# A long-convolution block and a gated FFN on one core: block 2's spectrum by n mod 4, warm-up products on a constant, diagonals by VectorE, the last rows in three pieces

## The chip, the cores and the metric

The kernel runs on one core of a Trainium2 chip. The metric is the device time of one execution in microseconds (us), taken on the device. Three runs of the kernel before gave 263.92, 263.94 and 264.01 us; the median is 263.94. Beside these there is one profiled execution, from which all rows below come.

The engines are named as the profile names them: PE is TensorE (matrix products; PEld is its loading of weights), DVE is VectorE, ACT is ScalarE, POOL is GpSimd, SP is SyncE, which mostly issues DMAs. A queue in a row such as SPq or POOLq is the engine's DMA-issuing side. L337 is line 337 of the kernel.

## The reference

Inputs are q, k, v of 2048 x 640, a four-tap kernel per channel, a long kernel `ssm_k` of 640 x 2048, a per-channel weight `ssm_D`, and the three matrices of a gated FFN with 1728 hidden columns. All are bfloat16.

```
kv = shift_conv4(k) * v                       # four taps along the sequence, per channel
y  = causal_conv(kv, ssm_k) + kv * ssm_D      # length 2048, by real FFT of length 4096
h  = q + layernorm(q) * y
n  = layernorm(h)
out = h + (silu(n @ w_gate) * (n @ w_up)) @ w_down
```

## The kernel before

The sequence is cut into four blocks of 512 positions, numbered 0 to 3. A block's 512 rows lie as four interleaved groups: position 4p + r is partition p, group r (r = 0 to 3). The causal convolution of length 2048 is done block by block: the spectrum X_j of block j's `kv` and the spectrum G_j of block j of `ssm_k` (each a real transform of 512 values to length 1024) are made once as matrix products with a constant basis `WF`; H_j is a window of G_j and G_(j-1); the output block j is the inverse transform of the sum over i of X_i times H_(j-i).

The stages of block j are named, in the code, Lg, Lk, Lv, Lx (loads), g (transpose of `ssm_k`), G (its spectrum), h (window), k (the four-tap convolution and the product with v), X (its spectrum), m0 to mj (complex products and sums, on VectorE), n (statistics of the first layer norm), i (inverse transform, the product with the normed q, the sum h and the second norm's statistics), t (the normed rows, turned), and f (the FFN). The name is followed by the block, so X2 is the spectrum of block 2's `kv` and m22 is X_2 times H_0.

**A spectrum** (`transform`, L353). In the form "sub", each of four column groups c takes four row groups r with two halves of 320 columns: 8 products of 128x128 by 128x320 (L337) into one PSUM tile, evicted twice (L326: the even rows doubled, and the sum), and one subtraction over the whole width (L372) gives the other half of the frequencies. In the form "four" the symmetry of n mod 4 is used once more: for each of even and odd rows only two column groups are multiplied, with two row groups each (4 products a group), also evicted twice; the other two groups follow by half-width subtractions (L401, one each for even and odd), and two full-width operations (L405 for the difference, L408 for the sum) join even and odd. Where the name is in `ADDLO` the sum is a DMA that adds into its target, issued by POOL (L410, through `add_into`, L257). Which form a spectrum takes stands in the table `SUM`; a name in `DIRECT` takes neither, but a path with a further constant `minus`. Inverse transforms i2 and i3 have the form "four" too.

**The FFN** of a block (`ffn`, L865) takes the turned normed rows hT: gate and up products (L889 for whole groups of 256 hidden columns, L923 for the odd rest), Silu and a copy on ScalarE (L906, L912; L931, L932), their product on VectorE (L914, L933), and the down products (L956): per group of 128 rows 14 chunks by two halves of 320 columns. For blocks 0 to 2 the rows are copied by ScalarE and added to `out` by POOL's DMAs (L963); block 3 adds h on VectorE (L972; L974 for halves) and SP stores the result (L976). The very last group of 128 rows is done as two halves of 320 columns, both in one PSUM tile `ps` (L950), each with its own eviction and store.

**The start.** VectorE and POOL make an identity (L983, L986). TensorE runs 14 products of the identity with itself to warm up (`spin`, L990), turns the taps (L1002), runs 16 more, then transposes block 0's k (L529), runs 8 more and does the four-tap convolution as products with diagonal matrices (L554), 80 of them, 20 for each r. The 20 diagonals (five chunks c of 128 channels, four taps each) are the identity times a tap (L1010): chunks 0 to 2 by VectorE, 3 and 4 by POOL.

**The order.** Every operation is added to a `Plan` by the code's loops, with the engine, an assumed duration, and the buffers that it reads and writes, and so gets a number. The list `ORDER` then says in which order they are emitted. Each engine carries out its own operations in that order, and so do the DMA queues of SP, ScalarE and POOL. A negative number ~n means the operation n in its other form, mostly an eviction by VectorE in place of ScalarE. Buffers (`SLOTS`) are given out and taken back in this order too, so a load waits for the last reader of the buffer that it gets. `schedule` (L174) only checks and emits; the list itself was made by a search outside the kernel with the assumed durations (`Plan.TOOK` for DMAs by packet size, the numbers in `pe`, `act`, `dve`, and 660 for a transposing DMA, a "turn").

TensorE's queue mixes two kinds of work: that of the convolution of block j, which depends on VectorE, and the FFN of block j-1, which only needs its weights and hT.

Of the kernel before, what the change touches and what calls it, by code (L numbers as in the profile page):

```python
# [10 lines left out]
FP32 = mybir.dt.float32  # L11
BF16 = mybir.dt.bfloat16
# [35 lines left out]
SUM = {'X3': 'four', 'i2': 'four', 'i3': 'four', 'G3': 'four', 'G0': 'four'}  # L48
# [7 lines left out]
PAIRED = True  # L56
ORDER = [
# [75 lines left out]
class Plan:  # L133
    TOOK = {8: 9, 128: 13, 256: 18, 512: 28.5, 640: 33, 1024: 47, 1280: 57, 4096: 160, 5120: 199}
# [63 lines left out]
def kernel(ctx: ExitStack, tc: tile.TileContext, A_q, A_k, A_v, A_shift_k, A_ssm_k, A_ssm_D, B_x,  # L198
# [53 lines left out]
    def transfer(nbytes, fn, r, w):  # L252
        return plan.moved("turn", nbytes, 256, fn, r, w)
# [161 lines left out]
    def g_turned(g, drow=None):  # L415
# [19 lines left out]
        if drow:  # L435
            dve(480, lambda: nc.vector.tensor_add(ap(gT)[0:1, 0, :], ap(gT)[0:1, 0, :], ap(drow)[0:1, :]), [drow], [(gT, 0)])
# [82 lines left out]
    def turned_k(k, behind=None, table=None):  # L519
        if plan.block in KTURN:  # L520
            return k
# [343 lines left out]
    def ffn(j, hT, h, end=False, lead=0):  # L865
# [73 lines left out]
        for gi in range(lead, NGRP - 1):  # L939
            chunks((gi,), ROWS)  # L940
# [207 lines left out]
```

## Time and profile before

| | |
|---|---|
| median of three runs | 263.94 us (263.92 to 264.01) |
| the profiled execution's own time | 264.02 us |
| its span, first to last instruction | 262.3 us |
| TensorE clock granted | 1.00 in all slices |
| mean DMA rate over the span | 166 GB/s |
| SP's queue, share of 16 DMA engines | 56.2% |
| POOL's queue, share of 16 DMA engines | 14.7% |

How to read the rows. A row of instructions has start and duration in us, engine, line, operation, the tile written and read with shapes, a count, and in brackets the time the engine stood idle before it with what ended that. A row of groups has busy time in us and mean ns of one, then idle time before. A row of waits has the total us, the number and the longest. A row of the chain has start, us and what ran. The 40 digits are the span in equal slices of 6.56 us, in tenths. Durations of products are latencies and overlap; how fast they follow one another is read from the chain.

### The profile page before, as it was taken

How to read it: one execution, taken by the hardware profiler on the slowest of the kernel's cores; microseconds unless marked ns; L12 is line 12 of the kernel's file. 1: busy time of each engine (PE TensorE's matmuls, PEld its weight loads, DVE VectorE, ACT ScalarE, POOL GpSimd, SP SyncE). 2: the span in 40 equal slices, each digit the busy share in tenths (PEclk: the TensorE clock that was granted, in tenths of full speed). 3: DMA queues.
4: the chain of work that ended last, by engine and by line, in shares of the span. 5: the costliest groups of instructions: out<-in, count | busy, mean ns of one | idle time of the engine just before them, and what ended most of it. 6: DMA issues, size and time to landing. Idle time of an engine off the chain costs nothing.

```text
span 262.3 us, 4671 instructions
## 1 busy us (share of the span) xinstructions
PE 255.3 (97%) x1786; PEld 159.5 (61%) x1802; DVE 204.9 (78%) x296; ACT 168.4 (64%) x288; POOL 67.4 (26%) x84
## 2 busy tenths in 40 slices
PE   7999999999999999999999999999999999999994
PEld 7977786554665567755754467544447764444772
DVE  4589999999999999999999999999998401115022
ACT  3999999986495896668968887343696033434100
POOL 4440000029972300025050000599900022000000
PEclk9999999999999999999999999999999999999999
DMA  7999999728958999759998769699190498000003
GB/s 257 342 260 309 235 343 297 134 62 154 292 108 155 196 266 162 127 122 279 238 174 218 183 151 169 105 235 237 51 225 1 80 205 139 7 0 0 2 0 100
DMA packets 72066, 43.42 MB, mean 166 GB/s; under 512 B 30886, under 2 KB 69100, under 8 KB 72044
## 3 DMA queue, kind: packets, MB, share of 16 engines
q1 hardware_dynamic: 68066, 37.22, 56.2%
q0 software_dynamic: 3968, 5.90, 14.7%
q8 instruction: 14, 0.23, 0.4%
q14 instruction: 8, 0.07, 0.1%
q10 hardware_dynamic: 10, 0.01, 0.0%
HBM read 30.01 MB, written 4.59 MB: 132 GB/s over the span
## 4 chain that ended last, share of the span: by engine, by line
PE 92%; DVE 2%; DMA 2%; ACT 2%; issue 1%; POOL 0%
PE ps L889 39%; PE ps L956 23%; PE ps L337 12%; PE ps L554 6%; PE ps L779 5%; PE ps L923 5%; DMA out_dram<-big 2%; PE ps L995 2%; PE ps L529 1%; ACT S L326 1%; PE ps L432 1%; DVE row L793 1%; DVE big L806 0%; ACT big L828 0%; DVE row L974 0%
## 5 line engine op out<-in xcount | busy, mean ns | idle before, releaser
L889 PE MATMUL ps<-big,big 128*128 128x512 bf16 x465 | 106.9, 379 | 0.8
L889 PEld LDWEIGHTS <-big 128*128 128x128 bf16 x480 | 46.8, 98 | 52.3
L956 PE MATMUL ps<-wd,tT 128*128 128x320 bf16 x416 | 60.4, 299 | 0.8 <-DVE row L974 0.8
L956 PEld LDWEIGHTS <-tT 128*128 128x128 bf16 x416 | 40.7, 98 | 17.3 <-issue 1.0
L906 ACT ACTIVATE sg<-ps 128x1024 bf16<-128x1024 f32 (+1 forms) x28 | 26.8, 961 | 30.1 <-PE ps L889 26.6
L337 PE MATMUL ps<-big,WF 128*128 128x320 bf16 x240 | 39.6, 299 | 0.5 <-ACT big L326 0.2
L914 DVE TENSOR_TENSOR tT<-sg,sg 128x1024 bf16<-128x1024 bf16 (+1 forms) x25 | 16.0, 644 | 26.1 <-ACT sg L912 26.1
L645 DVE TENSOR_TENSOR S<-S,big 128x2560 bf16<-128x2560 bf16 x23 | 34.3, 1492 | 0.8
L644 DVE TENSOR_TENSOR big<-S,S 128x2560 bf16<-128x2560 bf16 x23 | 34.1, 1485 | 0.0
L337 PEld LDWEIGHTS <-WF 128*128 128x128 bf16 x240 | 23.2, 98 | 12.8 <-issue 1.6
L912 ACT CAST sg<-ps 128x1024 bf16<-128x1024 f32 (+1 forms) x25 | 23.5, 945 | 7.1 <-PE ps L889 6.8
L963 POOL DMA_DIRECT2D out_dram<-row x12 | 11.0, 1038 | 60.2 <-ACT row L962 60.2
L655 ACT ACTIVATE row<-big 128x640 bf16<-128x640 bf16 x32 | 23.7, 744 | 1.4 <-DVE big L806 1.1
L326 ACT CAST S<-ps 128x320 bf16<-128x320 f32 (+1 forms) x38 | 20.0, 575 | 3.2 <-PE ps L337 3.0
L554 PE MATMUL ps<-diag,kT 128*128 128x128 bf16 x320 | 19.0, 219 | 0.0
L554 PEld LDWEIGHTS <-kT 128*128 128x128 bf16 x320 | 18.3, 98 | 1.0 <-DVE kT L533 0.2
L326 ACT ACTIVATE big<-ps 128x640 bf16<-128x640 f32 (+1 forms) x25 | 15.7, 666 | 4.8 <-PE ps L337 4.7
L962 ACT CAST row<-ps 128x640 bf16<-128x640 f32 x12 | 8.3, 690 | 14.2 <-PE ps L956 10.7
L257 POOL DMA_DIRECT2D S<-big x2 | 2.6, 1296 | 57.5 <-DVE big L639 30.7
L708 ACT ACTIVATE row<-big,sm 128x640 bf16<-128x640 bf16 x19 | 17.1, 939 | 0.0
L923 PE MATMUL ps<-big,big 128*128 128x512 bf16 x59 | 14.5, 379 | 0.1
L793 DVE SCALAR_TENSOR_TENSOR row<-row,ps 128x640 bf16<-128x640 bf16 x16 | 12.7, 813 | 0.0
(95 smaller groups left out, 300.5 us busy)
## 6 DMA issues: line engine op xcount, KB each, us to landing
big<-in_B_w_gate_dram SPq DMA_DIRECT2D x24, 320.0 KB, 5.1
big<-in_B_w_up_dram SPq DMA_DIRECT2D x24, 320.0 KB, 4.7
big<-in_A_q_dram SPq DMA_DIRECT2D x4, 640.0 KB, 5.1
big<-in_A_v_dram SPq DMA_DIRECT2D x4, 640.0 KB, 5.1
big<-in_A_ssm_k_dram SPq DMA_DIRECT2D x4, 640.0 KB, 7.8
wd<-in_B_w_down_dram SPq DMA_DIRECT2D x1, 2080.0 KB
out_dram<-big SPq DMA_DIRECT2D x3, 640.0 KB, 5.6
out_dram<-row POOLq DMA_DIRECT2D x12, 160.0 KB, 5.5
```

What stands on the lines that cost most here:

```text
L326: (lambda: nc.scalar.activation(dst(), src(), ACT.Copy, scale=2.0)) if twice else (lambda: nc.scalar.copy(dst(), src())),
L337: nc.tensor.matmul(ap(ps)[:, h, 0:NH], w, ap(src)[:, r, h * NH:(h + 1) * NH], start=(first and i == 0), stop=(last and i == len(rs) - 1), ...
L554: nc.tensor.matmul(line(ap(ps))[:, c * P:(c + 1) * P], ap(kT)[:, c, q, off:off + P], ap(diag)[:, 4 * c + t, :], start=(t == 0), stop=(t == 3))
L644: nc.vector.tensor_mul(flat2(b), X.part(xs), H.part(hs))
L645: f(A.part(dst), A.part(dst), flat2(b))
L655: act(825, lambda r=r, junk=junk: nc.scalar.activation(ap(junk), ap(x)[:, r, :], ACT.Square, scale=D ** -0.5, accum_out=sm(s, 1)[:, r:r + ...
L708: nc.scalar.activation(ap(row), ap(x)[:, r, :], ACT.Identity, bias=sm(s, 5)[:, r:r + 1], scale=sm(s, 4)[:, r:r + 1])
L889: nc.tensor.matmul(of(ps, i), ap(w)[:, k, off:off + P], ap(hT)[:, k, lo:lo + n], start=(k == 0), stop=(k == KT - 1))
L906: act(1010 if wide else 600, lambda: nc.scalar.activation(of(sg), of(*gate), ACT.Silu), [(gate[0], gate[1] + i) for i in range(m)], [sg])
L912: op = plan.add("act", 1010 if wide else 590, lambda: nc.scalar.copy(of(co), of(*up)), psu + [sg], [co] + tt, (), ("dve", 1230 if wide els ...
L923: nc.tensor.matmul(ap(ps)[:, i, :], ap(w)[:, k, off:off + P], ap(hT)[:, k, :], start=(k == 0), stop=(k == KT - 1))
L956: nc.tensor.matmul(ap(ps)[:, hf, 0:NH], t, ap(wd)[:, c, hf * NH:(hf + 1) * NH], start=(c == order[0]), stop=(c == order[-1]))
```

## The change

1. `SUM`: X2 takes the form "four", G0 leaves the table.
2. `spin`: with `EARLY` the warm-up products take a constant of ones in place of the identity, and don't depend on the identity.
3. `DIAGDVE = 4`: chunks 0 to 3 of the diagonals are made by VectorE, chunk 4 by POOL.
4. `LASTCUT`: the last group of 128 rows is done in three pieces of 320, 160 and 160 columns. The third has a PSUM tile of its own (`other`). The chunks of its products are cut at 4 and 8 instead of 5 and 10.
5. A turn is assumed to take 1000 instead of 660 in the plan, the diagonals get other assumed durations, a packet size of 320 is added, and `ORDER` is a new list with 914 operations for 906.

The other new names (`K0TURN`, `FFN4`, `KVPAIR`, `DPOOL`) are switched off, and what they call is not run: `by_four`, `whole`, `odd_by_four`, block 0's k by transposing DMAs, kv in pairs of rows. It is left out below.

```diff
-SUM = {'X3': 'four', 'i2': 'four', 'i3': 'four', 'G3': 'four', 'G0': 'four'}
+SUM = {'X3': 'four', 'X2': 'four', 'i2': 'four', 'i3': 'four', 'G3': 'four'}
...
+K0TURN = False
+EARLY = True
+FFN4 = False
+KVPAIR = ()
+DPOOL = False
+LASTCUT = True
+DIAGDVE = 4
 ORDER = [
-    1, 32, 0, 2, 13, 16, 4, 17, 5, 18, 7, 6, 25, 21, 27, 9, 11, 19, 3, 26, 8, 23, 24, 190, 29, 31, 124, 10, 12, -29, -31, 218,
...
-    893, 894, 895, 899, 884, 885, 901, 904, 905, 896, 898, 900, 902, 903]
+    1, 0, 4, 2, 3, 5, 7, 12, 8, 13, 9, 6, 15, 11, 14, 10, 27, 28, 23, 16, 127, 24, 122, 32, 124, 121, 17, 18, 19, 25, -27, 29, 31,
...
+    892, 884, 905, 885, 893, 898, 908, 909, 886, 900, 887, 903, 906, 888, 910, 911, 904, 907, 912, 913, 811]
...
-    TOOK = {8: 9, 128: 13, 256: 18, 512: 28.5, 640: 33, 1024: 47, 1280: 57, 4096: 160, 5120: 199}
+    TOOK = {8: 9, 128: 13, 256: 18, 320: 21, 512: 28.5, 640: 33, 1024: 47, 1280: 57, 4096: 160, 5120: 199}
...
-        op = self.add(eng, 660.0 if eng == "turn" else n * self.TOOK[packet] / 16 * (2.1 if eng == "add" else 1.0), fn, reads, writes)
+        op = self.add(eng, 1000.0 if eng in ("turn", "aturn") else n * self.TOOK[packet] / 16 * (2.1 if eng == "add" else 1.0), fn, reads, writes)
...
-            cuts = [0, 5, 10, NCH]
             last = end and r == ROWS[-1]
+            cuts = [0, 4, 8, NCH] if last and LASTCUT else [0, 5, 10, NCH]
+            parts = [((0, 1), 0, NH)] if not last else [((0,), 0, NH), ((1,), 0, NH // 2), ((1,), NH // 2, NH // 2)] if LASTCUT else [((0,), 0, NH), ((1,), 0, NH)]
+
+            other = new("ps_f") if last and LASTCUT else ps
+
+            def of(hs, to, n):
+                return [(other if to else ps, frozenset((hf, x) for hf in hs for x in range(to, to + n, NH // 2)))]
             for lo, hi in zip(cuts, cuts[1:]):
-                for hs in ((0,), (1,)) if last else ((0, 1),):
-                    def mm(r=r, ps=ps, cs=order[lo:hi], hs=hs, order=order):
+                for hs, to, n in parts:
+                    def mm(r=r, ps=other if to else ps, cs=order[lo:hi], hs=hs, order=order, to=to, n=n):
...
                             for hf in hs:
-                                nc.tensor.matmul(ap(ps)[:, hf, 0:NH], t, ap(wd)[:, c, hf * NH:(hf + 1) * NH],
-                                                 start=(c == order[0]), stop=(c == order[-1]))
+                                nc.tensor.matmul(ap(ps)[:, hf, to:to + n], t, ap(wd)[:, c, hf * NH + to:hf * NH + to + n],
+                                                 start=(c == order[0]), stop=(c == order[-1]), skip_group_check=True)
...
-            for hs in ((0,), (1,)) if last else ((0, 1),):
-                n = NH * len(hs)
-                lo = hs[0] * NH
...
+            for hs, to, n in parts:
+                lo = hs[0] * NH + to
+                n = n * len(hs)
...
         def go():
+            ones = nc.const_aps.tensor(1.0, [P, P], BF16) if EARLY else ap(ident)
             for _ in range(n):
-                nc.tensor.matmul(ap(warm)[:, 0, 0:P], ap(ident), ap(ident), start=True, stop=True)
-        return pe(56 * n, go, [ident], [warm])
+                nc.tensor.matmul(ap(warm)[:, 0, 0:P], ones, ones, start=True, stop=True)
+        return pe(56 * n, go, [] if EARLY else [ident], [warm])
...
-        def fill(c=c, v=nc.vector if c < 3 else nc.gpsimd):
+        def fill(c=c, v=nc.vector if c < DIAGDVE else nc.gpsimd):
...
-        plan.add("dve" if c < 3 else "pool", 650 if c < 3 else 1300, fill, [ident, taps], [(diag, c)])
+        plan.add("dve" if c < DIAGDVE else "pool", 745 if c < DIAGDVE else 2450, fill, [ident, taps], [(diag, c)])
```

What the new order does near the places above, read from both lists: VectorE's operations of the same kinds between the first m00 product and the last row combination of i3 number 150 in both; TensorE's four products of i3 for the group r = 0 that came last in the old list come first in the new one; in the last rows the first piece's products come early, its eviction follows, 18 products of another row stand between that and the second piece, and the third piece comes last.

More of the change, by code (lines that the diff above doesn't have):

```diff
@@ L506, in load_k @@
     def load_k(j):
-        if j in KTURN:
+        if j in KTURN or not j and K0TURN:
             kT = new("kT")
             for r in range(R):
-                transfer(MB / 4, lambda r=r: nc.sync.dma_start(
-                    out=ap(kT)[:, :, r, PAD:], in_=block(kk, j)[:, r, :], transpose=True), [], [(kT, r)])
+                q, e = (nc.scalar, "aturn") if not j and r % 2 else (nc.sync, "turn")
+                transfer(MB / 4, lambda r=r, q=q: q.dma_start(
+                    out=ap(kT)[:, :, r, PAD:], in_=block(kk, j)[:, r, :], transpose=True), [], [(kT, r)], e)
             return kT
@@ L519, in turned_k @@
     def turned_k(k, behind=None, table=None):
-        if plan.block in KTURN:
+        if plan.block in KTURN or not plan.block and K0TURN:
             return k
@@ L546, in kv_of @@
         kv = new("t4")
-        for r in range(R):
+        for r in (0, 2, 1, 3) if plan.block in KVPAIR else range(R):
             ps = conv_ps()
@@ L561, in straight @@
                 nc.vector.tensor_mul(ap(kv)[:, r, :], line(ap(ps)), rd(v)[:, r, :])
-            if plan.block >= ACTKV:
+            if plan.block in KVPAIR:
+                act(700, lambda r=r, ps=ps: nc.scalar.copy(ap(kv)[:, r, :], line(ap(ps))), [ps], [(kv, r)])
+                if r > 1:
+                    dve(820, lambda r=r: nc.vector.tensor_mul(ap(kv)[:, r - 2::2, :][:, 0:2], ap(kv)[:, r - 2::2, :][:, 0:2], rd(v)[:, r - 2::2, :][:, 0:2]), [v], [(kv, r - 2), (kv, r)])
+            elif plan.block >= ACTKV:
                 op = plan.add("act", 700, lambda r=r, ps=ps: nc.scalar.copy(ap(kv)[:, r, :], line(ap(ps))), [ps, v], [(kv, r)], (), ("dve", 820, straight))
@@ L896, in chunks, with by_four, whole, mm @@
             return last
+        fours = []
+        def by_four(gi):
+            if not gi % 2:
+                fours.append(new("co"))
+            co, c, at = fours[-1], 2 * gi, 2 * (gi % 2)
+            for i, (w, off) in enumerate(load_w(gi)):
+                ps = new("ps_f")
+                for k in range(2):
+                    last = whole(ps, k, w, off + k * P)
+                src = [(ps, 0), (ps, 1)]
+                if i:
+                    act(1010, lambda ps=ps: nc.scalar.copy(ap(co)[:, at:at + 2, :], ap(ps)), src, [(co, gi % 2)])
+                else:
+                    act(1010, lambda ps=ps: nc.scalar.activation(ap(tT)[:, c:c + 2, :], ap(ps), ACT.Silu), src, [done(range(c, c + 2), ROWS)])
+            if gi % 2:
+                dve(1220, lambda: nc.vector.tensor_mul(ap(tT)[:, c - 2:c + 2, :], ap(tT)[:, c - 2:c + 2, :], ap(co)), [co], [done(range(c - 2, c + 2), ROWS)])
+            return last
+        def whole(ps, i, w, off):
+            def mm():
+                for k in range(KT):
+                    nc.tensor.matmul(ap(ps)[:, i, :], ap(w)[:, k, off:off + P], ap(hT)[:, k, :], start=(k == 0), stop=(k == KT - 1))
+            return pe(1080, mm, [w, hT], [(ps, i)], [tT], 418)
+        def odd_by_four():
+            w = load_w(NGRP - 1)[0][0]
+            co, ps = new("co"), new("ps_f")
+            whole(ps, 0, w, 0)
+            whole(ps, 1, w, P)
+            c = NC_FULL - 1
+            act(600, lambda ps=ps: nc.scalar.activation(ap(tT)[:, c, :], ap(ps)[:, 0, :], ACT.Silu), [(ps, 0)], [done((c,), ROWS)])
+            act(590, lambda ps=ps: nc.scalar.copy(ap(co)[:, 0, :], ap(ps)[:, 1, :]), [(ps, 1)], [(co, 0)])
+            dve(420, lambda: nc.vector.tensor_mul(ap(tT)[:, c, :], ap(tT)[:, c, :], ap(co)[:, 0, :]), [(co, 0)], [done((c,), ROWS)])
+            ps = new("ps_f")
+            last = whole(ps, 0, w, 2 * P)
+            act(600, lambda ps=ps: nc.scalar.activation(ap(tail)[0:64, :], ap(ps)[0:64, 0, :], ACT.Silu), [(ps, 0)], [done_tail(ROWS)], [tT])
+            act(590, lambda ps=ps: nc.scalar.copy(ap(co)[0:64, 1, :], ap(ps)[64:P, 0, :]), [(ps, 0)], [(co, 1)])
+            dve(420, lambda: nc.vector.tensor_mul(ap(tail)[0:64, :], ap(tail)[0:64, :], ap(co)[0:64, 1, :]), [(co, 1)], [done_tail(ROWS)], [tT])
+            return last
         def gate_up(c, m, gate, up, sg, co, lo, n, rs):
@@ L939, in ffn @@
         for gi in range(lead, NGRP - 1):
-            chunks((gi,), ROWS)
-        behind = odd_chunks()
+            by_four(gi) if FFN4 else chunks((gi,), ROWS)
+        behind = odd_by_four() if FFN4 else odd_chunks()
         for gi in range(0, lead, 2):
@@ L955, in mm @@
                             for hf in hs:
-                                nc.tensor.matmul(ap(ps)[:, hf, 0:NH], t, ap(wd)[:, c, hf * NH:(hf + 1) * NH],
-                                                 start=(c == order[0]), stop=(c == order[-1]))
+                                nc.tensor.matmul(ap(ps)[:, hf, to:to + n], t, ap(wd)[:, c, hf * NH + to:hf * NH + to + n],
+                                                 start=(c == order[0]), stop=(c == order[-1]), skip_group_check=True)
                     rows = [done(order[lo:hi], (r,))] + ([done_tail((r,)), (tail, "zero")] if NC_FULL in order[lo:hi] else [])
-                    pe(136 * (hi - lo) * len(hs), mm, [wd] + rows, [(ps, hf) for hf in hs]).deps.add(behind)
+                    pe(136 * (hi - lo) * len(hs) * n // NH, mm, [wd] + rows, of(hs, to, n)).deps.add(behind)
             o = new("o")
@@ L1034 @@
     k = turned_k(k, spun, table)
-    again = spin(WARMUP[2])
-    again.deps.update(op for op in plan.ops if op.name == "k0" and op.eng == "pe" and op is not again)
+    again = spun
+    if not K0TURN:
+        again = spin(WARMUP[2])
+        again.deps.update(op for op in plan.ops if op.name == "k0" and op.eng == "pe" and op is not again)
     kv = kv_of(0, k, None, v, again)
```

18 lines of the change are left out of this document (10 added, 8 removed), and 68 rows, old and new, of the table ORDER.

## The prediction

> **What bounds the kernel now.** I read the busy times and their slices first, then TensorE's waits, then VectorE's long stretch, then the place where the two engines meet.
>
> ```profile
> PE 255.3 (97%) x1786; PEld 159.5 (61%) x1802; DVE 204.9 (78%) x296; ACT 168.4 (64%) x288; POOL 67.4 (26%) x84
> DVE  4589999999999999999999999999998401115022
> ...
> PE ps L995 <- POOL ident L986: 1.6, 1, 1.6
> PE ps L956 <- DVE row L974: 0.8, 1, 0.8
> ```
>
> TensorE works from 1.56 us to the end and waits for two things that count: the identity at the start (1.6) and VectorE's L974 at the end (0.8). The chain of waits, which is nearly all PE, only repeats that TensorE's queue is full. But VectorE is full too, from slice 4 to about 200 us, and the time can hang on either.
>
> ```profile
> 21.15:196.29 175.14, 173.85 (x1202) 106.11 (x1214) 172.64 (x221) 134.02 (x222) 54.79 (x51) 1.00 0.85 193
> ...
> 21.15 0.83 DVE L617 TENSOR_TENSOR S<-S,S 128x1280 bf16<-128x1280 bf16 x1 [0.15 <-ACT S L326]
> ...
> 194.73 1.56 DVE L759 TENSOR_TENSOR S<-big 128x1280 bf16<-128x1280 bf16 x2
> ...
> 196.92 1.25 PE L779 MATMUL ps<-S,WI 128*128 128x320 bf16 x8
> ...
> 213.76 0.38 PE L889 MATMUL ps<-big,big 128*128 128x512 bf16 x1
> ```
>
> From the first spectral product (L617) to the last row combination of block 3's inverse (L759, ends 196.29) VectorE is busy 172.64 of 175.14 us (the columns of the first row after the length are PE, PEld, DVE, ACT, POOL). The inverse's eight products (L779) that need this result start at 196.92, only 0.63 us later. So 196.29 is the meeting point: work taken from TensorE before it is worth 0.63 at most, unless VectorE arrives earlier too. Behind it TensorE alone sets the end.
>
> **Block 2's spectrum by n mod 4.** Four column groups with 8 products each become four with 4: 16 products fewer.
>
> ```profile
> 52.35 0.54 PE ps L337 x4
> ...
> L645 DVE TENSOR_TENSOR S<-S,big 128x2560 bf16<-128x2560 bf16 x23 | 34.3, 1492 | 0.8
> L401 DVE TENSOR_TENSOR big<-S,big 128x1280 bf16<-128x1280 bf16 x1 | 0.8, 818 | 0.0
> L561 DVE TENSOR_TENSOR big<-ps,big 128x640 bf16<-128x640 f32 x6 | 4.9, 822 | 2.2 <-PE ps L554 2.2
> L564 DVE TENSOR_TENSOR big<-big,big 128x640 bf16<-128x640 bf16 x10 | 4.7, 484 | 0.0
> L705 DVE TENSOR_SCALAR row<-big,sm 128x640 bf16<-128x640 bf16 x13 | 5.2, 441 | 0.0
> ...
> S<-S POOLq DMA_DIRECT2D x2, 640.0 KB, 7.4
> ```
>
> TensorE saves 4 x 0.54 = 2.16 us. On VectorE one full-width subtraction stays (L404 for L372, the size of an L645, 1.49) and two of half width are added (L401, 0.82): +1.64. The evictions stay eight. The new order pays most of this back: numbering the operations as the kernel adds them and reading both lists, VectorE has 150 of them from its first m00 product to that last L759, before as after. One L561 became an L564 behind a ScalarE copy (-0.34); one L705 (-0.44) and one eviction copy (0.49, the size of the L434 shown below) went to ScalarE. Sum for VectorE: 1.64 - 1.27 = **+0.37**. ScalarE, busy 134 of 175 us in this stretch, hides what it takes over; without that cover VectorE would stand for the same amount.
>
> The sum of the even and the odd part (X2 is in ADDLO) becomes a DMA that accumulates, from POOL's queue. It is first read by m22. Between lie, on VectorE, two multiply-and-add pairs of m12 (1.49 + 1.49 each), four L705 and a norm: 7.7 us without the norm, against a landing in 7.4. I cost it at nothing; from there on VectorE stands, and each us is an us of the end. POOL has only the copy of block 3's halo directly ahead of it. Dropping G0 from the table changes nothing, since G0 takes the DIRECT branch.
>
> **The start.**
>
> ```profile
> 0.94 0.07 DVE kT L542
> ...
> 1.56 1.68 PE ps L995 x14
> 3.23 0.23 PE ps L1002 x4
> 3.46 1.82 PE ps L995 x16
> 5.28 2.13 PE ps L529 x20
> ...
> 8.00 4.54 PE ps L554 x78
> ...
> 123.95 3.35 PE ps L554 x60
> ...
> kT<-in_A_k_dram SPq DMA_DIRECT2D x1, 640.0 KB, 4.0
> ...
> 0.81 0.40 SPq L516 DMA_DIRECT2D kT<-in_A_k_dram  x1
> ...
> 3.80 2.23 DVE L1010 TENSOR_SCALAR diag<-ident,taps 128x128 bf16<-128x128 bf16 x12
> 3.87 4.94 POOL L1010 TENSOR_SCALAR diag<-ident,taps 128x128 bf16<-128x128 bf16 x8 [2.37 <-DVE taps L1006]
> ```
>
> The warm-up products now need only a constant, so they can begin when VectorE does, about 0.94: 0.62 earlier. The 34 products ahead of the transposes take 1.68 + 0.23 + 1.82 = 3.73, to 4.67; but block 0's k was issued at 0.81 and landed 4.0 later, at 4.81. So the transposes start at about 4.9 for 5.28: -0.38. The first convolution takes 4.54 for 78 products; at the later rate (3.35 for 60) it would be 4.35. I put the 0.19 down to the fifth chunk's diagonals, which POOL ended at 8.81. With four chunks on VectorE (another 2.23/3 = 0.74, where it would wait for the transposes) POOL has one, 2.5 us, and the 0.19 goes. The convolution ends 0.57 earlier. Behind it the order gives VectorE two evictions more (some 0.49 each) ahead of its first L617, against waits of 0.55, 0.33 and 0.15 there:
>
> ```profile
> 15.34 0.49 DVE L329 TENSOR_SCALAR big<-ps 128x320 bf16<-128x320 f32 x1 [0.55 <-ACT big L326]
> ...
> 17.04 0.49 DVE L434 COPY big<-ps 128x640 bf16<-128x640 bf16 x1 [0.33 <-PE ps L432]
> ```
>
> Bounds: all of the 0.98 is paid, 0.41 later; none, and half the waits go as well, 1.0 earlier. I take **0.4 earlier**: the waits' rows show room for most of it.
>
> TensorE's rate doubles between the transposes and 8.00: 106 ns a product in them, 58 in the 78 behind. The Trainium skill (TensorE: Matmul & The Clock Gate, What's actually happening) says that the gate opens after one busy window of 3.4 us, and that the windows run free. By that rule an earlier start could open it a window sooner; the transposes would take half as long, VectorE's diagonals and evictions would then set the convolution's start, and the sum would be some 0.5 lower, an estimate from that page and the rows above. One trace with one opening can't say.
>
> **The meeting point in the new order.** VectorE: 196.29 - 0.4 + 0.37 = 196.26, and a product follows within 0.05: 196.3 for 196.92, **-0.6**. TensorE is there earlier and waits. The order also puts four more products of the inverse (0.54) ahead of this point, which leaves **-0.54** behind it.
>
> **The end.**
>
> ```profile
> 257.19 2.08 PE ps L956 x14
> 259.27 0.02 issue
> 259.29 0.49 DVE row L974
> ...
> L972 DVE TENSOR_TENSOR row<-ps,big 128x640 bf16<-128x640 f32 x3 | 2.4, 821 | 9.7 <-PE ps L956 9.7
> L554 PEld LDWEIGHTS <-kT 128*128 128x128 bf16 x320 | 18.3, 98 | 1.0 <-DVE kT L533 0.2
> ...
> out_dram<-row SPq DMA_DIRECT2D x3, 160.0 KB, 1.8
> out_dram<-row SPq DMA_DIRECT2D x2, 80.0 KB, 1.6
> ```
>
> The second half of the last row's products waited for the eviction of the first half, which lies in the same PSUM tile. In the new order 18 products of another row (L956, 2.4 us) stand between, more than an eviction of 0.49, and the third piece has a tile of its own: **-0.82**; 0 if the wait returns. The last eviction covers 160 columns for 320; 320 take 0.49 and 640 take 0.82, so by the slope 0.32: **-0.16**. Its DMA halves: **-0.1** (0 to -0.2, from 1.8 and 1.6). 28 products of 160 columns replace 14 of 320; 128 columns take 56 ns, so 160 about 69, 1.93 for 1.90: **+0.05** (+0.84 if each took the 98 ns that a weight load is busy; the 60 above, each with its own load, show that it doesn't).
>
> The Trainium skill (same page, LDWEIGHTS) gives a weight load as its columns over 1.2 GHz, 107 ns. By that the 28 would take 3.0 and the sum would be 1.1 higher; this trace has 56 ns for a load and its product together.
>
> Sum: -0.6 - 0.54 - 0.82 - 0.16 - 0.1 + 0.05 = -2.2. The profiled execution took 264.02 (1.72 of it around the span), 0.08 over the runs' median: 264.02 - 2.2 = **261.8**.
>
> **Rivals.** *TensorE sets it all.* If VectorE gets well ahead (full rate comes sooner, the evictions fit into the waits), TensorE's whole saving counts: -2.16 - 0.62 - 0.82 - 0.16 - 0.1 + 0.05 = -3.8, **260.2**. For it: TensorE is busy 173.85 of the 175.14 as well. Against: the 0.63 at the meeting point.
>
> *VectorE falls back.* The order is new everywhere, and each new wait of VectorE moves the 196.3. With its start 0.41 late and one us of new waits it is 1.8 more, 263.6; in the middle **262.9**. For it: TensorE now waits at that point, so nothing takes up a loss. Against: the list has the same 150 operations.
>
> *Slower: block 3's turned rows come late.*
>
> ```profile
> 204.00 1.51 DVE L705 TENSOR_SCALAR row<-big,sm 128x640 bf16<-128x640 bf16 x4
> ...
> 204.51 5.24 SPq L819 DMA_TRANSPOSE big<-row  x4
> ...
> DMA to landing us min/median/max: 2.6/2.7/3.7
> ...
> L914 DVE TENSOR_TENSOR tT<-sg,sg 128x1024 bf16<-128x1024 bf16 x21 | 14.4, 686 | 24.4 <-ACT sg L912 24.4
> ```
>
> The FFN of block 3 can't begin before four transposing DMAs (L819) have landed. In the new order one more L914 (0.69) stands ahead of the norm that they wait for, so the first goes out near 205.2, the last three times 1.31 later, 209.1, and lands 2.7 later at 211.8. TensorE asks at 213.76 - 0.6 - 0.54 = 212.6. The margin is 0.8, from there each us is an us. Rows that land at 215.3 or later make the kernel slower by over 0.5; at 215.6, **264.8**. For it: on SP's queue three weight loads stand directly ahead of these DMAs, and they wait for buffers. Against: TensorE, whose f2 work frees those buffers, is there before.
>
> *The change doesn't do what it says* where the eviction wait returns in the last row: **262.6**.
>
> **How the numbers follow.** VectorE paces, 261.2 to 262.6: 0.5. TensorE paces, 260.2 to 261.2: 0.15. VectorE falls back, or the last row waits, 262.6 to 263.4: 0.18. Within 0.2% (0.53 us, about what a measurement of this kernel can tell from no change): 0.05. Slower: 0.12. So faster is 0.83. The range, 260.4 to 263.6, leaves out the slower case and the tip of the fast one.
>
> **What would show it.** Right: the first L995 near 0.9; 224 products of L337 with WF for 240; VectorE from its first L617 to its last L759 of block 3 in 175.5 us; L779 within 0.1 of that; no wait of TensorE in the last row; a final eviction of 0.32. Wrong: TensorE waiting for L819's DMAs near 212, VectorE waiting for POOL's DMA ahead of m22, or that L759 ending later than 196.9.

## The result, and the profile after

Five runs of the changed kernel have a median of 262.76 us (262.58 to 262.90), five of the kernel before beside them 263.92 (263.91 to 264.01). The ratio is 0.9954, with a 95% interval of 0.9940 to 0.9969: 1.2 us faster, where 2.1 to 2.2 were forecast. The profiled execution took 262.58 with a span of 260.9 (before: 264.02 and 262.3): these two differ by 1.4, a little more than the medians.

Lines have moved: L337 is now L344, L554 L564, L617 L631, L744 L758, L759 L773, L779 L793, L889 L903, L956 L1019, L972 and L974 L1035 and L1037, L995 L1059, L1002 L1066. First the busy times and VectorE's slices of the kernel after.

```profile
PE 254.3 (97%) x1800; PEld 158.0 (61%) x1800; DVE 206.4 (79%) x303; ACT 170.1 (65%) x289; POOL 68.7 (26%) x81
...
DVE  5599999999999999999999999999999501032132
```

From its view of windows, the stretch from VectorE's first L631 to its last L773 (the columns as in the prediction):

```profile
21.26:196.39 175.13, 173.71 (x1203) 105.01 (x1201) 172.71 (x221) 135.62 (x223) 57.61 (x51) 1.00 0.88 191
```

The row is nearly the one of before (175.14, PE 173.85, VectorE 172.64): both engines are full, and VectorE starts 0.1 later, not 0.4 earlier. The timeline of the kernel after has the later point where the two meet, and the end.

```profile
194.16 1.42 PE L793 MATMUL ps<-S,WI 128*128 128x320 bf16 x8
...
194.83 1.56 DVE L773 TENSOR_TENSOR S<-big 128x1280 bf16<-128x1280 bf16 x2
...
196.49 0.71 PE L793 MATMUL ps<-S,WI 128*128 128x320 bf16 x4
...
204.63 5.41 SPq L833 DMA_TRANSPOSE big<-row  x4
...
213.11 5.13 PE L903 MATMUL ps<-big,big 128*128 128x512 bf16 x23
...
257.70 0.32 DVE L1037 TENSOR_TENSOR row<-ps,big 128x160 bf16<-128x160 f32 x1 [0.37 <-PE ps L1019]
```

Read against before: the product that needs VectorE's last row combination comes at 196.49 for 196.92 (0.43 earlier), block 3's FFN begins at 213.11 for 213.76 (another 0.22), the final eviction at 257.70 for 259.29 (0.94 more), and the span ends 3.20 after that, for 3.01 (0.19 given back). 0.43 + 0.22 + 0.94 - 0.19 = 1.40, the whole difference of the spans (which are given to 0.1, so the last term is good to some 0.05). The turned rows (L833) went out by 210.1 and nobody waited for them.

One place of before was not looked at in the prediction: the first product of block 2's inverse, i2, where VectorE and TensorE meet earlier. From the timeline of the kernel before:

```profile
129.16 1.56 DVE L744 TENSOR_TENSOR S<-S 128x1280 bf16<-128x1280 bf16 x2
...
131.49 1.25 PE L779 MATMUL ps<-S,WI 128*128 128x320 bf16 x8
```

And of the kernel after:

```profile
129.58 1.55 DVE L758 TENSOR_TENSOR S<-S 128x1280 bf16<-128x1280 bf16 x2
...
131.43 0.71 PE L793 MATMUL ps<-S,WI 128*128 128x320 bf16 x4
```

VectorE's results (L744, now L758) are there by 130.72 before and by 131.13 after, so TensorE comes last at i2 in both kernels, by 0.77 and by 0.30. TensorE had 16 products fewer ahead of this point (2.16) and gained 0.06. The weight loads up to there, one a product, say why: of L337 there are 16 fewer (208 for 224 with WF), but of L889 there are five more (185 for 180), products of 512 columns of block 1's FFN that the new order drew ahead, 1.08. The other 1.0 is lost time. Most of it lies between 40 and 60 us. The windows there, of the kernel before and then of the kernel after (the first number behind the length is PE's busy time):

```profile
40.00:60.00 20.00, 19.40 (x132) 11.39 (x132) 19.59 (x30) 17.75 (x34) 2.61 (x3) 1.00 0.75 158
```

```profile
40.00:60.00 20.00, 18.75 (x130) 10.92 (x127) 19.59 (x29) 17.73 (x34) 3.81 (x4) 1.00 0.75 210
```

And TensorE's waits in the kernel after:

```profile
PE ps L564 <- ACT kT L543: 0.6, 1, 0.6
PE ps L1066 <- DMA row<-in_A_shift_k_dram: 0.5, 1, 0.5
PE ps L344 <- ACT big L333: 0.4, 1, 0.4
PE ps L439 <- ACT big L842: 0.3, 2, 0.2
```

Before the FFN of block 0 can begin (48.91 after, 47.32 before), TensorE has only products whose inputs or PSUM tiles come straight from ScalarE and VectorE, and in the new order it stands 1.25 us there, 0.65 more than before (the last two of these waits lie there). From 60 us to 194 no wait of it is listed in either kernel.

### The profile page after: what moved, and what is told of

It reads as the page before. It is cut to its first block, busy times and chain, and to the rows that moved or that the text cites. A ratio compares the mean times of both kernels' runs of the same rounds, so it can differ in the third digit from the quotient of the medians.

```text
span 260.9 us, 4685 instructions
## 1 busy us (share of the span) xinstructions
PE 254.3 (97%) x1800; PEld 158.0 (61%) x1800; DVE 206.4 (79%) x303; ACT 170.1 (65%) x289; POOL 68.7 (26%) x81
## 4 chain that ended last, share of the span: by engine, by line
PE 83%; DVE 9%; ACT 4%; DMA 2%; issue 1%; SPq 0%; DVEq 0%
PE ps L903 40%; PE ps L1019 23%; PE ps L344 5%; PE ps L564 5%; PE ps L980 5%; PE ps L793 3%; DVE S L631 2%; DMA big<-in_A_q_dram 2%; DVE row L807 1%; ACT big L842 1%; ACT big L333 1%; ACT S L333 1%; DVE big L631 1%; DVE S L336 1%; DVE big L738 1%
## 5 line engine op out<-in xcount | busy, mean ns | idle before, releaser
L903 PE MATMUL ps<-big,big 128*128 128x512 bf16 x480 | 108.2, 379 | 0.2 <-ACT big L842 0.2
L903 PEld LDWEIGHTS <-big 128*128 128x128 bf16 x480 | 46.8, 98 | 52.7 <-issue 0.3
L1019 PE MATMUL ps<-wd,tT 128*128 128x320 bf16 (+1 forms) x429 | 60.3, 295 | 0.0
L1019 PEld LDWEIGHTS <-tT 128*128 128x128 bf16 x429 | 41.3, 98 | 16.4 <-issue 0.4
L344 PE MATMUL ps<-big,WF 128*128 128x320 bf16 x224 | 36.5, 299 | 0.8 <-ACT big L333 0.4
L969 ACT CAST sg<-ps 128x1024 bf16<-128x1024 f32 (+1 forms) x25 | 24.2, 966 | 10.6 <-PE ps L903 9.5
L344 PEld LDWEIGHTS <-WF 128*128 128x128 bf16 x224 | 21.7, 98 | 11.7 <-issue 1.2
L669 ACT ACTIVATE row<-big 128x640 bf16<-128x640 bf16 x32 | 23.9, 753 | 2.6 <-DVE big L820 2.5
L264 POOL DMA_DIRECT2D S<-big x3 | 3.8, 1261 | 63.4 <-DVE S L412 25.2
L564 PE MATMUL ps<-diag,kT 128*128 128x128 bf16 x320 | 19.5, 219 | 0.6 <-ACT kT L543 0.6
L564 PEld LDWEIGHTS <-kT 128*128 128x128 bf16 x320 | 18.6, 98 | 2.2 <-ACT kT L543 0.7
L333 ACT CAST S<-ps 128x320 bf16<-128x320 f32 (+1 forms) x34 | 17.8, 586 | 1.0 <-PE ps L344 0.5
L722 ACT ACTIVATE row<-big,sm 128x640 bf16<-128x640 bf16 x20 | 17.9, 951 | 0.5 <-DVE sm L676 0.5
L333 ACT ACTIVATE big<-ps 128x640 bf16<-128x640 f32 (+1 forms) x22 | 13.0, 656 | 4.9 <-PE ps L344 4.8
L968 DVE TENSOR_TENSOR tT<-sg,ps 128x1024 bf16<-128x1024 bf16 (+1 forms) x3 | 3.1, 1043 | 15.4 <-PE ps L903 14.4
L980 PE MATMUL ps<-big,big 128*128 128x512 bf16 x60 | 14.7, 379 | 0.0
```

The source lines that it names most:

```text
L333: (lambda: nc.scalar.activation(dst(), src(), ACT.Copy, scale=2.0)) if twice else (lambda: nc.scalar.copy(dst(), src())),
L344: nc.tensor.matmul(ap(ps)[:, h, 0:NH], w, ap(src)[:, r, h * NH:(h + 1) * NH], start=(first and i == 0), stop=(last and i == len(rs) - 1), ...
L564: nc.tensor.matmul(line(ap(ps))[:, c * P:(c + 1) * P], ap(kT)[:, c, q, off:off + P], ap(diag)[:, 4 * c + t, :], start=(t == 0), stop=(t == 3))
L669: act(825, lambda r=r, junk=junk: nc.scalar.activation(ap(junk), ap(x)[:, r, :], ACT.Square, scale=D ** -0.5, accum_out=sm(s, 1)[:, r:r + ...
L722: nc.scalar.activation(ap(row), ap(x)[:, r, :], ACT.Identity, bias=sm(s, 5)[:, r:r + 1], scale=sm(s, 4)[:, r:r + 1])
L903: nc.tensor.matmul(of(ps, i), ap(w)[:, k, off:off + P], ap(hT)[:, k, lo:lo + n], start=(k == 0), stop=(k == KT - 1))
```

## The experiments

Each was timed in five rounds beside the kernel before (263.92 to 263.95). Positions of single profiled executions scatter by some 0.2 us; for times the intervals are given.

**The start.** Why does VectorE not begin earlier? In the kernel after the four-tap products (L564) wait for ScalarE's second eviction of kT, and that stands behind a statistic (L669) of 0.74. The timeline of the kernel after:

```profile
0.85 1.65 PE L1059 MATMUL ps<-const-bfloat16-1.0 128*128 128x128 bf16 x14 [0.85 <-PEq L1198]
...
4.91 1.95 PE L539 MATMUL ps<-ident,kT 128*128 128x128 bf16 x20
...
6.42 0.74 ACT L669 ACTIVATE row<-big 128x640 bf16<-128x640 bf16 x1
7.15 0.67 ACT L543 COPY kT<-ps 128x640 bf16<-128x640 bf16 x1
...
7.88 4.64 PE L564 MATMUL ps<-diag,kT 128*128 128x128 bf16 x80 [0.56 <-ACT kT L543]
```

The first experiment puts the eviction ahead of the statistic:

```diff
-    ... 27, 28, 23, 16, 127, 24, 122, 32, ...
+    ... 27, 28, 23, 16, 24, 127, 122, 32, ...
```

> The changed kernel with one exchange in ScalarE's order at the start: the second eviction of block 0's turned k stands ahead of the first statistic of x (L669), which waits for x's load. Theory (the start's gain was lost behind that wait): the eviction runs right behind the first one, at 6.36 instead of 7.15, VectorE's two evictions (6.62 to 7.51) are then the last, the four-tap products start near 7.55 instead of 7.88, VectorE's first L631 comes 0.3 earlier than 21.26, and the time falls by 0.3, to 262.4. Rival (the start doesn't count, the stretch from 21 to 196 us is held by loads and ScalarE): the products start earlier but the first L631 stays within 0.1 and the time within 0.1.

The second also moves VectorE's fill of the fourth chunk's diagonals (operation 11) behind its two evictions of kT.

> As the kernel with the eviction first, and VectorE makes the fourth chunk's diagonals behind its two evictions instead of ahead of them. Theory (what holds the four-tap products is the last of four evictions): VectorE's evictions move from 6.62 to about 6.4, the products start near 7.35, 0.5 earlier than in the changed kernel, and the time is 262.25. Rival: the fourth chunk's diagonals (0.74) now come too late for the thirteenth product and the same wait stands inside the first 20 products; time as with the eviction first.

The third of this group takes the warm-up back to the identity (in its order the first warm-up then stands behind the making of the identity):

```diff
-EARLY = True
+EARLY = False
```

> The changed kernel with the warm-up products on the identity again, as before. Theory (the start of the four-tap products is set by ScalarE's statistic, not by TensorE): the first product moves from 0.85 to about 1.5, the products start within 0.1 of 7.88 and the time within 0.15. Rival (the earlier warm-up is worth what it is early): 0.4 to 0.6 slower, 263.2.

Measured: 263.01 (ratio 0.9966, 0.9953 to 0.9979), 263.12 (0.9965, 0.9952 to 0.9978) and 262.72 (0.9955, 0.9943 to 0.9967). All three intervals overlap that of the kernel after. The timeline of the first:

```profile
0.84 1.65 PE L1060 MATMUL ps<-const-bfloat16-1.0 128*128 128x128 bf16 x14 [0.84 <-PEq L1199]
...
5.07 2.17 PE L540 MATMUL ps<-ident,kT 128*128 128x128 bf16 x20
...
7.55 4.90 PE L565 MATMUL ps<-diag,kT 128*128 128x128 bf16 x80
7.86 4.42 PEld L565 LDWEIGHTS <-kT 128*128 128x128 bf16 x79 [0.27 <-DVE kT L544]
...
21.27 0.82 DVE L632 TENSOR_TENSOR big<-S,S 128x1280 bf16<-128x1280 bf16 x1
```

The first four-tap product starts at 7.55 for 7.88, but the second weight load waits until 7.86 for VectorE's eviction of kT. So the products end only 0.07 earlier (12.45 for 12.52), and VectorE's first spectral product stands where it stood, 21.27. With the identity they start at 8.00 and that product at 21.39:

```profile
1.49 1.67 PE L1060 MATMUL ps<-ident 128*128 128x128 bf16 x14 [1.49 <-POOL ident L1050]
...
5.00 1.59 PE L540 MATMUL ps<-ident,kT 128*128 128x128 bf16 x20
...
8.00 4.64 PE L565 MATMUL ps<-diag,kT 128*128 128x128 bf16 x80 [0.88 <-ACT kT L544]
...
21.39 0.83 DVE L632 TENSOR_TENSOR big<-S,S 128x1280 bf16<-128x1280 bf16 x1
```

So the warm-up on a constant is worth nothing here. VectorE does follow the products: its first operation on them (L571) starts at 9.27 in the kernel after, at 9.19 with the eviction first and at 9.39 with the identity, and the 0.12 of the last stays up to 21.39. But neither trace ends the convolution much earlier, and the kernel before had this operation at 9.27 too and the end at 12.53. So what an earlier end would be worth was not tried. The 0.08 of the first experiment is still there at 20.32 (L380) and gone at 21.27; what takes it was not traced.

**Which engine paces.** Four experiments take work from one engine or both. Twelve FFN products of block 1 out, from the kernel after and from the kernel before:

```diff
                     for k in range(KT):
+                        if j == 1 and gis[0] < 3 and k == 2:
+                            continue
```

> The kernel after, with 12 products of block 1's FFN left out (the third of five row chunks in the gate and up products of the first three groups of 256 hidden columns): 2.6 us less for TensorE, ahead of block 3's inverse, so the output of block 1 is not the reference's. Theory (VectorE paces the long stretch): VectorE still needs its 172.7 us, ends L773 within 0.3 of 196.4, and the time falls by 0.3 or less: 262.4 to 262.8. Rival (TensorE is the pace, and VectorE only looks full because it is fed just in time): the time falls by most of 2.6, to 260.2 to 260.8.

> The kernel before, with the same 12 products of block 1's FFN left out: 2.6 us less for TensorE. The prediction's premise: work taken from TensorE ahead of the meeting point is worth 0.63 at most, so 263.3 to 263.9. Rival (TensorE was the pace of the kernel before): 261.3 to 261.9.

Two of the four additions of m13 out, and then both together:

```diff
-                f(A.part(dst), A.part(dst), flat2(b))
+                if at != (3, 1) or xs:
+                    f(A.part(dst), A.part(dst), flat2(b))
```

> The kernel after, with two of the four additions of m13 left out (block 3's sum then lacks a term): 2 x 1.49 = 3.0 us less for VectorE in the long stretch. Theory (VectorE paces, with TensorE right behind it): TensorE is busy 173.7 of the 175.1 us, so only its 1.4 us of waits there can go: the time falls by 0.7 to 1.4, to 261.4 to 262.1, and TensorE sets the meeting point. Rival 1 (VectorE alone is the bound): it falls by 2.6 to 3.0, to 259.8 to 260.2. Rival 2 (VectorE doesn't pace): no change, 262.6 to 262.9.

> The kernel after with both relieved: the 12 FFN products of block 1 and two of m13's additions left out (2.6 us less for TensorE, 3.0 us less for VectorE). Theory (two engines level within 0.5 us; each relief alone gave 0 and 0.5): together 1.8 to 2.6 below after, 260.2 to 261.0. Rival (a third bound: loads, evictions by ScalarE): less than 1 below after, 261.8 or more.

| left out | median us | against after (262.76) |
|---|---|---|
| TensorE 2.6 us, ahead of i2 | 262.93 | +0.17 |
| VectorE 3.0 us, behind i2 | 262.24 | -0.52 |
| both | 262.23 | -0.53 |
| TensorE 2.6 us, in the kernel before | 266.39 | (+2.5 against before) |

With both, the time falls by no more than with the one alone. The theory had 1.8 to 2.6; the number is inside the rival's range, but the rows show no third bound. The relief of TensorE came out 0.13 above its theory's range. That of VectorE lies between its theory and its second rival, and the interval of its ratio (0.9926 to 0.9951) still touches that of the kernel after, so its 0.5 is not well determined. The timeline and the waits say more. With less for TensorE it comes to i2 early and stands there, because VectorE sets that point:

```profile
131.33 0.72 PE L793 MATMUL ps<-S,WI 128*128 128x320 bf16 x4 [1.51 <-DVE S L758]
```

With both relieved it is the same, TensorE's largest wait being

```profile
PE ps L794 <- DVE S L759: 1.8, 1, 1.8
```

again at i2. m13 lies behind i2. There the relieved VectorE runs ahead, and TensorE sets the rest; the windows of the kernel with less for VectorE alone, over its stretch from VectorE's first spectral product to its last row combination:

```profile
21.41:195.32 173.91, 172.49 (x1198) 104.67 (x1196) 169.86 (x218) 134.36 (x222) 57.83 (x51) 1.00 0.88 192
```

And its timeline:

```profile
196.47 0.71 PE L794 MATMUL ps<-S,WI 128*128 128x320 bf16 x4
...
212.77 1.46 PE L904 MATMUL ps<-big,big 128*128 128x512 bf16 x6
```

VectorE's last row combination ends 1.1 earlier (195.32), but the product behind it starts at 196.47 for 196.49, and block 3's FFN only 0.34 earlier. So in the kernel after the two are nearly level at both points. At i2 TensorE is last by 0.30, and relieved of 2.6 it stands there for VectorE. Behind i2 TensorE paces, with VectorE right behind it: relieved there, VectorE gives some 0.5 us at most.

In the kernel before, less work for TensorE made it slower. Its waits:

```profile
PE ps L779 <- DVE S L744: 2.3, 1, 2.3
...
DVE S L744 <- DMA S<-S: 2.6, 1, 2.6
```

And its windows around i2 (the third number from the end is the granted clock):

```profile
130.00:132.00 2.00, 0.21 (x1) 0.00 (x0) 0.33 (x1) 2.00 (x4) 0.00 (x0) 1.00 1.15 256
132.00:134.00 2.00, 1.43 (x7) 0.75 (x8) 2.00 (x4) 1.61 (x4) 0.00 (x0) 0.80 1.10 255
134.00:136.00 2.00, 2.00 (x7) 0.76 (x5) 2.00 (x5) 0.00 (x0) 0.00 (x0) 0.50 0.13 31
136.00:138.00 2.00, 2.00 (x12) 1.19 (x11) 1.90 (x4) 0.00 (x0) 1.75 (x2) 0.85 0.24 38
```

VectorE waits for the accumulating DMA that POOL issues for i2 (S<-S). It went out at 121.2 as before but landed after 10.5 us, where the longest of this line took 7.5; then TensorE stood 2.3, then had half its clock for about 3.4 (2.3 + 1.7, and 1.1 of waiting for kT behind POOL at another place, against the 2.6 saved). That this DMA was slowed by loads that a faster TensorE had released sooner fits, but was only argued. This experiment therefore doesn't say what TensorE's work was worth in the kernel before.

**Block 2's spectrum alone.** Taken out of the kernel after, the rest of the new order kept; and put alone into the kernel before, its operations where the old ones stood:

```diff
-SUM = {'X3': 'four', 'X2': 'four', 'i2': 'four', 'i3': 'four', 'G3': 'four'}
+SUM = {'X3': 'four', 'i2': 'four', 'i3': 'four', 'G3': 'four'}
...
-SUM = {'X3': 'four', 'i2': 'four', 'i3': 'four', 'G3': 'four', 'G0': 'four'}
+SUM = {'X3': 'four', 'X2': 'four', 'i2': 'four', 'i3': 'four', 'G3': 'four', 'G0': 'four'}
```

> The kernel after with block 2's spectrum back in its old form, all other operations in the order of after: TensorE gets 16 products more (2.16 us, 175.9 in a stretch of 175.1), VectorE 1.64 us less (171.1). Theory (TensorE and VectorE were nearly level, and the new form moved work between them): TensorE is then the longer and the time rises by 0.7 to 1.5, to 263.4 to 264.3. Rival (VectorE alone paces, so the new form cost its 1.64): the time falls, to 261.1 to 262.3.

> The kernel before with one part of the change, block 2's spectrum by n mod 4, its operations put where the old form's stood: 16 products less (2.16 us) for TensorE, 1.64 us more for VectorE, and nothing given to ScalarE. Theory (VectorE paces, so the new form alone costs, and only the new order's shifts to ScalarE make it pay): 264.7 to 265.6. Rival (TensorE paces before as well, as the kernel after with the old form suggests): 261.8 to 263.4.

Without it: 265.20 (ratio 1.0045, 1.0032 to 1.0057), 2.44 above the kernel after, more than theory allowed. The point i2 moves by all that TensorE has more:

```profile
133.71 0.71 PE L793 MATMUL ps<-S,WI 128*128 128x320 bf16 x4
```

131.43 + 2.16 = 133.6: TensorE had no slack at i2, and what VectorE saved bought nothing. So the rest of the change, this part left out, is slower than the kernel before although its last row is better: the new order spends on FFN products and on lost time what the 16 products leave free. (It was made for the new form; an order made for the old one was not tried.)

Alone in the old order: 272.30 (1.0315, 1.0299 to 1.0332), far beyond the 265 expected, for another reason than VectorE's 1.64 us. The waits of that kernel:

```profile
PE ps L889 <- DMA big<-row: 6.6, 1, 6.6
...
DVE big L644 <- DMA S<-big: 6.4, 1, 6.4
```

And its windows, the clock again third from the end:

```profile
114.00:116.00 2.00, 0.00 (x0) 0.00 (x0) 2.00 (x3) 0.00 (x0) 0.00 (x0) 0.63 0.93 134
116.00:118.00 2.00, 0.00 (x0) 0.00 (x0) 1.97 (x2) 0.00 (x0) 0.00 (x0) 0.50 0.47 88
118.00:120.00 2.00, 1.59 (x4) 0.58 (x5) 2.00 (x2) 0.00 (x0) 0.00 (x0) 0.50 0.00 0
```

The sum of even and odd is a DMA (S<-big), and in the old order m22 reads it right behind. VectorE stands 6.4; the last of block 1's normed rows is queued behind the waiting L644, so its turning is late and TensorE stands 6.6, then works at half its clock.

**The end.** The second and third piece stored by one DMA with rows of 640 bytes; then two pieces in one PSUM tile, the other row's products still between them; then those products moved ahead, so that the second half follows the first at once:

```diff
+                if last and (hs, to) == ((1,), 0):
+                    plan.ops[-1].fn = None
+                if last and to:
+                    plan.ops[-1].fn = lambda r=r, o=o: nc.sync.dma_start(out=block(oo, j)[:, r, NH:D], in_=ap(o)[:, NH:D])
...
-LASTCUT = True
+LASTCUT = False
...
-            cuts = [0, 4, 8, NCH] if last and LASTCUT else [0, 5, 10, NCH]
+            cuts = [0, 4, 8, NCH] if last else [0, 5, 10, NCH]
...
-    ... 884, 903, 885, 893, 898, 905, 906, 886, 900, 887, ...
+    ... 884, 885, 886, 903, 893, 898, 905, 906, 900, 887, ...
```

> The changed kernel with the second and third piece of the last rows stored by one DMA of 320 columns (640 bytes a row) behind the third eviction, in place of two of 160. Theory (rows of 320 bytes are acknowledged later: 0.87 between the last packet and SP's drain against 0.43 before): the drain comes 1.7 behind the issue instead of 1.95, the time falls by 0.2 to 0.3, to 262.5. Rival (the longer closing is chance, or comes from two DMAs close together): the time stays within 0.1 or rises by 0.1, since twice the bytes follow the last eviction.

> The kernel after with the last row in two pieces of 320 columns, both in one PSUM tile, as before; the products of another row stay between them. Theory: the distance between the pieces removed the wait of 0.8, not the third piece; the final eviction is 0.49 for 0.32, but the last store goes out as one with rows of 640 bytes and closes about 0.3 to 0.4 sooner: no wait of TensorE in the last row, and the time is 0.3 below to 0.1 above that of after (262.4 to 262.9). Rival (the third piece and its own tile did it): the wait returns, 263.3 to 263.7.

> As the two-halves kernel, but all three parts of the other row's products go ahead of the first half's last products, so that the second half follows the first at once, as before. Theory: TensorE waits for the eviction of the first half again, 0.8, and the time is 0.8 above that of the two-halves kernel. Rival (the 0.95 that after gains behind f3's first product is not this wait): within 0.2 of it.

Measured: 262.52 (ratio 0.9958, 0.9943 to 0.9972), 262.69 (0.9954, 0.9941 to 0.9968) and 263.61 (0.9982, 0.9974 to 0.9991). With two halves no product of the last row waits; with the old neighbourhood the wait is back, and the time is 0.92 higher, of which the wait itself is 0.6 and 0.28 stood already ahead of the last rows (248.81 for 248.53 at the same products of the two profiled executions):

```profile
PE ps L1019 <- DVE row L1037: 0.6, 1, 0.6
```

What the third piece does lies between the final eviction and the end. The final evictions of the one-store kernel and of the two halves:

```profile
257.92 0.33 DVE L1037 TENSOR_TENSOR row<-ps,big 128x160 bf16<-128x160 f32 x1 [0.37 <-PE ps L1019]
```

```profile
257.96 0.49 DVE L1037 TENSOR_TENSOR row<-ps,big 128x320 bf16<-128x320 f32 x1 [1.08 <-PE ps L1019]
```

Their spans end at 260.8 and 261.0, 2.88 and 3.04 after these starts; the kernel after, with a short eviction and two stores, takes 3.20. So the short eviction is worth 0.16 and the second store costs 0.32. The other kernels with the second store agree: 3.14 to 3.23. SP's wait for the last store was 0.8 in the kernel before and is 1.1 in the kernel after:

```profile
SPq L1143 <- DMA out_dram<-row: 0.8, 1, 0.8
```

```profile
SPq L1209 <- DMA out_dram<-row: 1.1, 1, 1.1
```

The trace shows what the 0.32 is, and it is not the store. From its issue to SP's release the last store takes 1.50 with 160 columns, and 1.60 to 1.62 with 320 (the kernels before, with one store and with two halves). From the last packet to that release it is 0.37 to 0.39 in all of them, so the small rows are not acknowledged later: the theory of the one-store kernel had the right number for a wrong reason. But SP closes the kernel by waiting for its semaphores one after another, some 0.06 apart. With two stores the last one's semaphore is second in that row, and 0.5 of further waits follows its release; with one store it stands at the row's end, and 0.07 follows.

The one-store kernel has the lowest median of all that compute everything, but its interval overlaps that of the kernel after: a gain of 0.3 in the closing is shown in the profile, one in the time isn't.

## Why the prediction was half right

The sign and the cause of the largest gain were right; the sum of -2.2 came out at -1.40 in the span. Every sign that the prediction named for being right came, from the first product near 0.9 to the final eviction of 0.32; none of them tested the start of VectorE or the point i2, where the forecast went wrong. By its steps:

- *The start, 0.4 earlier.* Wrong. The first product came at 0.85 and the transposes at 4.91, as forecast, but the four-tap products at 7.88 for 7.70 and VectorE's first L631 0.11 later. The step that failed is the convolution's end, forecast 0.57 earlier: it came at 12.52 for 12.53, because the first products wait for the evictions of kT by ScalarE and VectorE and not for TensorE. What an earlier end would give VectorE stays open.
- *The 0.19 that POOL's fifth diagonals were to cost.* Wrong. With one chunk left, POOL ended at 6.35, and the 80 products still took 4.64 us, 58 ns each as before.
- *The clock's opening.* The 20 transposes took 2.17, 1.95 and 1.59 us with first products at 0.84, 0.85 and 1.49, so an earlier start did not bring the full rate sooner. The Trainium skill's sentence (TensorE: Matmul & The Clock Gate, What's actually happening) that the windows run free, so that the point of change varies, agrees with these three. None of them moved the time.
- *VectorE's work, +0.37.* Oversized: its busy time rose by 0.07 in a stretch of the same length.
- *The meeting point, -0.6.* Measured -0.43, but not for the reason given. "TensorE is there earlier and waits" failed: it arrived level, since of its 2.16 us it kept only 0.06 at i2. The prediction had one meeting point; i2 is an earlier one, and it stayed at 131.4. Behind it TensorE saved the 1.08 us of FFN products that the new order had drawn ahead of i2, less the 0.54 of the four products of the next step.
- *Four products ahead of it, -0.54.* Measured -0.22. There was no wait ahead of the meeting point to move them into, so they only changed sides. With less work for VectorE this stretch takes 16.30, the full 0.54 less than the 16.84 of before; in the kernel after, TensorE's weight loads still stand 0.3 for VectorE's last row combination. That accounts for about half of the missing 0.32, and the rest was not traced.
- *X2's sum by DMA, at nothing.* Right: no wait of VectorE for it. Without its cover, in the old order, VectorE stood 6.4 us and the time rose by 8.35: more than the us for an us of the prediction, with TensorE at half its clock behind the standing.
- *The eviction's wait, -0.82.* Right, and for the reason given, the 18 products between: two halves in one tile don't wait either. Behind block 3's first FFN product the gain to the final eviction was 0.94 (the extra 0.12 wasn't traced), and putting the wait back cost 0.92 in time, with a wait of 0.58.
- *The final eviction, -0.16, and the narrow products, +0.05.* Right: 0.32, and 69 ns a product as forecast: 24 of the 28 start from 255.84 to 257.43 (four had run further ahead). The loads' own time does not space them. The Trainium skill (TensorE: Matmul & The Clock Gate, LDWEIGHTS) gives a weight load as its columns over 1.2 GHz, 107 ns for 128. Here a load is busy for 98 ns, and it overlaps the products.
- *The last DMA, -0.1.* Right for the DMA itself: 1.50 for 1.62 from its issue to SP's release. What the sum lacked is what follows: SP's closing waits, 0.5 for 0.07 behind that release, so the tail grew by 0.19 in place of shrinking by 0.26.

Of the rivals, block 3's turned rows did not come late; VectorE did not fall back behind i2; TensorE does set the end from i2 on, but without the 2.2 us that the 260.2 needed. What sets VectorE's arrival at i2, 0.41 later than before (0.11 of it its later start), and whether relieving both engines in the half where each paces would add up, was not tried.

## What to carry to other kernels

Where two full engines hand work to each other several times, find every point where they meet and say for each which one arrives last, and by how much: work saved on the last is worth no more than that distance, and work saved on the first is lost at the next meeting. A DMA whose result is read on the engine that waits needs its landing time in other work behind it, and everything queued behind the wait is late as well. A wait for a buffer is removed by putting foreign work between as well as by a further buffer; a smaller last piece has to earn its own store, and with it what the closing of the kernel does behind that store.

## What the runs showed of the hardware

A standing of TensorE for 2.34 us was followed by half the clock for about 3.4 us, beginning 0.6 after work had resumed (kernel before with less work for TensorE; windows of half a us show 0.50 from 133.5 to 136.5); standings of 1.5 and 1.8 us left it at 1.00. The Trainium skill (TensorE: Matmul & The Clock Gate, Why this matters for your kernels) warns of gaps above some 3 us; here a shorter one was enough, once. A wait can therefore be dearer than its length: this one cost some 2.3 + 1.7.

A store of 40 KB with rows of 320 bytes released SP 1.50 us after its issue, one of 80 KB with rows of 640 bytes 1.60 to 1.62 us (kernel after; kernels before, with one store and with two halves). SP's closing waits ended some 0.06 us apart, so a store whose semaphore stands early in that row delays the end by all that stand behind it, some 0.5 us in the kernel after.
